# Three more inner fifth products, later sums and another order of the first down pass in a layer of linear attention and gated ReGLU

## Chip, cores and metric

The kernel runs on one core of a Trainium2 chip. The metric is device time in microseconds (us) of one execution; before the change the median of 3 runs is 710.93 us (710.85 to 712.28). The profiled execution took 711.03 us, of which the profile's span is 709.3 us.

## What is computed

`A_x` is 2048 x 1024 in bf16. The layer is a pre-norm linear attention block and a pre-norm feed-forward block, each with a residual:

```
q, k, v = split(layernorm(x) @ wqkv)            # 32 heads of 32
pq, pk  = phi(q), phi(k)                         # phi(t) = where(t > 0, t + 1, exp(t)) + 1e-6
o       = (pq @ (pk^T v)) / (pq @ sum(pk) + 1e-6)
h       = x + o @ wo
n       = layernorm(h)
gate    = n @ W_gate                             # 1024 x 3584
out     = h + (relu(gate) * (n @ W_up)) @ W_down # 3584 x 1024
```

The change touches the feed-forward block alone.

## The kernel before

**Engines and plan.** The program is written as one list of instructions for each engine; a small planner (`_Plan`) adds the semaphore waits from what each instruction reads and writes (`_Buf`; `over` names the buffers that lived at the same address before). Each engine works its list in order. TensorE (PE) multiplies, VectorE (DVE) and ScalarE (ACT) clear PSUM banks and make sums, GpSimd (POOL) makes some sums, SyncE (SP) issues nearly all DMAs.

**Products by sums.** Large products are done by a scheme of the Strassen-Winograd kind: a 2 x 2 block product takes seven block products P1 to P7 instead of eight, with sums of the operands (S1 to S4 of the activations, T1 to T4 of the weights) and sums of the results. A block product here is a stationary 128 x 128 block of weights and 512 moving columns, with four steps of the contraction and two column blocks `u`: 8 matmuls of 512 columns. The same scheme can be used once more inside a block product ("inner"): seven inner products M1 to M7, each 2 matmuls of 256 columns, so 14 matmuls of 256 columns.

**Passes and units.** The tokens are worked in two passes of 1024 (index 0 and 1; "pass 1" in the title of the change is the first one, index 0). A pass has 14 units (`ffn_unit`, line 1728, NPAIR = 14), each of which makes two tiles of the hidden layer (128 rows each) for gate (even unit) or up (odd unit); an odd unit multiplies its result into that of the even unit before it. Then comes a down pass (`down_pass`, line 2033) with W_down.

Inside a unit, two block products can be inner:
- The fifth product P5 (S1 times T1), as M1 to M7, in units of `M0` (line 1722: 4, 6, 8, 10) in the first pass, in all units of the second. It needs sums of quarters of S1 (`x_inner`, once a pass, tile `xs5`) and of T1 (`w_inner`, once a unit, tile `g5`), both in the region RE.
- The first product P1 of the next unit, as R1 to R7 beside the products of this one, if `inner1` of the next unit holds (line 1725); it needs sums of quarters of the raw weights (`w_inner1`, tile `g1`), and VectorE adds Ra at the end. It is left out for unit 0 of both passes and for unit 2 of the first (`NO_R`, line 1723).

VectorE's other work in a unit: the sums T for the next unit (`t_sums`, line 1626: T13, T2, T4, or T1, T2, T4, T3 when split), the evacuations "c22" and "c12" from PSUM, the multiplications h11, h21, h2 of an odd unit, "s5a" of an inner P5. In the first pass it also makes the sums of W_down that the down pass will need (`wd_pair`, line 820, instructions WT; `wl_sums`, line 850, WL, two of whose sums GpSimd makes); they are stored to DRAM (`t_scr`, `r_scr`, `l_scr`). Beside these run, in the first pass, the layer norms of the second half of the tokens (`late_steps`, line 1576: mean, square, norm for each of 8 tiles, on ScalarE with three small GpSimd steps after the square), one or two steps a unit in the places `lna` and `lnb`. The normalised tiles go to DRAM (`n_scr`) and come back transposed: four early, by a DMA transpose in units 11 to 13 into the tile `hnE` (line 286), from where ScalarE copies them into place at the start of the down pass (`early_c`); four in the down pass (`late_t`).

A unit's places are lists of such steps that `ffn_unit` calls between its products: `pre`, `wina`, `winb`, `lna`, `lnb`, `tail`, `mid`, `winc`. They set the order on each engine.

**Down pass.** It has seven products (index `pi` 0 to 6) on sums of the hidden tiles: D1, D2, D3 and D4. D1 is the sum of the second half's columns of an even and an odd tile, D3 the difference of the halves of an even tile (both by `hh_pair`, line 1662, two tiles at a time), D2 = D1 less the first half of the even tile, D4 the first half of the odd tile less D2. In the first down pass products 0 and 2 are direct (`direct`, 56 matmuls of 512 columns), the others are inner ("level two": `level2`, 98 matmuls of 256 columns in seven sets), each with sums of quarters of its own: sg6 for product 1, sg7 for 3, sg5 for 4, sg4 for 5, sg3 for 6. The PSUM banks are used in two halves of four, XB and YB. Weights come through a ring of 7 slots; `load_wd_next` issues the next load on SP when a slot is given back. `ORDER` (line 708) is the order of the weights, the calls of `direct` and `level2` (from line 2271) that of the products, and `at(pi, ci, ...)` places a step behind chunk `ci` of product `pi`.

D1 lives in the region RXH (7 x 1024 columns of 2 bytes, 512 columns a tile), `hnE` before the change in the last half of the eight blocks of RE, where `xs5` and `g5` are too:

```
hnE = RE[:, 4 * D:8 * D].rearrange("p (t a c) -> p t a c", t=STB, c=P)      # line 286
D1  = RXH[:].bitcast(f16).rearrange("p (q t) -> p q t", t=SBW)
```

So before the change no unit after the tenth could use `xs5` and `g5`.

Of the kernel before, what the change touches and what calls it, by code (L numbers as in the profile page):

```python
# [132 lines left out]
def bass_sequential_preLN__linear_attn_block__glu_gated_reglu__prompt_kernel(  # L133
# [71 lines left out]
    with es:  # L205
# [79 lines left out]
        g5 = RE[:, 6 * D:8 * D].bitcast(f16).rearrange("p (s j c) -> p s j c", s=2, j=4)  # L285
        hnE = RE[:, 4 * D:8 * D].rearrange("p (t a c) -> p t a c", t=STB, c=P)
        o0 = (NO + NOE) * D
# [50 lines left out]
        RXH = sb("RXH", [P, (NXN + NHS) * D], bf16)  # L338
        xn = RXH[:, 0:NXN * D].rearrange("p (a b) -> p a b", a=NXN)
        TWo_x = RXH[:, 0:KH * D].bitcast(f16).rearrange("p (j k c) -> p j k c", j=2, k=KH)  # L340

# [239 lines left out]
        for b_ in B_D1:  # L581
            b_.over = B_xn + B_TWo[0::2] + B_hs + hp_x
        for b_ in B_Ef:
# [13 lines left out]
        for b_ in B_hnE:  # L597
            b_.over = B_o + B_oT[0:NOE]
        for b_ in B_hnE:
            b_.over = b_.over + B_xs5 + flat(B_g5)  # L600
        for b_ in B_xs5 + flat(B_g5):
            b_.over = B_o + B_oT[0:NOE]
        for b_ in B_V:
            b_.over = B_hnE
        for b_ in flat(B_hh) + B_out2:
# [1020 lines left out]
        def t_sums(L, eng="dve", split=False):  # L1626
# [30 lines left out]
            if eng == "dve":  # L1657
                return [add13] + add(1, wb(1, 1), tb(0), 0) + add(3, wb(1, 0), tb(1), 1)
            return (add(0, wb(0, 1), wb(0, 0)) + add(1, wb(1, 1), tb(0), 0) + add(2, wb(1, 1), wb(0, 1)) +
                    add(3, wb(1, 0), tb(1), 1))  # L1660

        def hh_pair(q):
            f1, f2, f3 = 2 * q, 2 * q + 1, 2 * q + 4
            t0, t1 = slice(0, SBW), slice(SBW, 2 * SBW)
            PL.add("dve", lambda e: e.tensor_tensor(out=D1[:, q:q + 2, :], in0=hh[:, f1:f3:2, t1],
                                                    in1=hh[:, f2:f3:2, t1], op=ALU.add),
                   reads=[B_hh[f][1] for f in range(f1, f3)], writes=B_D1[q:q + 2], name="D1_%d" % q)
            PL.add("dve", lambda e: e.tensor_tensor(out=hh16[:, f1:f3:2, t1], in0=hh[:, f1:f3:2, t0],
                                                    in1=hh[:, f1:f3:2, t1], op=ALU.subtract),
                   reads=[B_hh[f][0] for f in (f1, f1 + 2)], writes=[B_hh[f][1] for f in (f1, f1 + 2)],  # L1670
                   name="D3_%d" % q)

# [360 lines left out]
        def down_pass(ps_, fill):  # L2033
# [138 lines left out]
            def direct(pi, bk, act_ops, start, evac):  # L2172
                af, ab = act_ops
                for ci, (q0, q1) in enumerate(WCH):
                    def go(ci=ci, q0=q0, q1=q1):
# [119 lines left out]
            sg5 = l2_sums(q_d1, sgs[4], "sg5")  # L2295
            for i in range(4):
                at(1, 2 + i if not last else (2, 3, 4, 5)[i], sg7[i])
            if not last:
                at(0, 0, lambda: d2(0, NH), lambda: d2(NH, NPAIR))
                at(0, 1, sg6[0])  # L2300
                at(0, 2, *sg6[1:3])
                at(0, 3, sg6[3])
                for i in range(4):
                    at(2, 1 + i, sg5[i])
                claim(B_sgg, B_w[0:4])
                at(2, 2, lambda: d4(0, NH))
                for i in range(4):
                    at(2, 1 + i, sg4[i])
                at(3, 0, lambda: d4(NH, NPAIR))
            else:  # L2310
                claim(B_W, B_hnT)
# [340 lines left out]
        for p_ in range(NPASS):  # L2652
            done = []
            for q in range(NPAIR):
# [7 lines left out]
                if (p_, q) == (0, 0):  # L2662
                    pre.append(ss[3])
                if q > 1 and q % 2:
                    wina.append(lambda q=q: hh_pair(q - 3))
                if p_ == 0:
                    raw, lna, lnb, tail = [], [], [], []
                    if q > 0 and ln_q:
# [3 lines left out]
                        lna.append(f_)  # L2672
                        f_, t1 = ln_q.pop(0)
                        lnb.append(f_)
                        done = [t for t in (t0, t1) if t is not None and t < STB]
                    winc = []
# [31 lines left out]
                if q == 0:  # L2708
# [51 lines left out]
            if p_ + 1 < NPASS:  # L2760
# [83 lines left out]
```

## Time and profile before

| | us |
|---|---|
| median of 3 runs | 710.93 |
| profiled execution | 711.03 |
| its span | 709.3 |
| first unit of the first pass begins | 222.62 |
| first down pass begins | 389.05 |
| second pass begins | 466.80 |
| second down pass begins | 631.05 |

All times inside the span count from its start. The beginnings are starts of matmuls in PE's timeline: PE's rows stand in the order of the program, and every unit begins with the first matmul of a known product, so counting the rows of each form cuts the span into units. A window's "x69" counts rows that overlap it, one more than the unit's own 68. In the timeline a row's first number is its start and the second its length, for merged rows the length of all; a matmul's row lasts longer than the distance to the next one, since matmuls are pipelined. "SPq" rows are DMA issues on SP; their length is how long the issue held the queue.

### The profile page before, as it was taken

Reading aid. Unit: us, or ns where it says so; the run is one execution under the profiler, and the core shown is the slowest. Engines: PE = TensorE matmul, PEld = TensorE weight load, DVE = VectorE, ACT = ScalarE, POOL = GpSimd, SP = SyncE. Lnnn points to the kernel's source line nnn. Section 1 sums busy time; section 2 is a strip of 40 time slices with the busy share of each in tenths; the row PEclk is TensorE's granted clock in tenths of the full one; section 3 lists DMA queues with packets and bytes.
Section 4 is the critical chain, followed back from the end, with each engine's and each line's share of the span. In section 5 each row is a group of like instructions: output and inputs, shape, how many; then the busy total and the mean of one; then the engine's idle time right before and its main releaser. Section 6 shows DMA issues by size and latency. Waiting matters only on the chain.

```text
span 709.3 us, 13488 instructions
## 1 busy us (share of the span) xinstructions
PE 704.0 (99%) x5101; PEld 398.3 (56%) x5101; DVE 612.4 (86%) x970; ACT 409.6 (58%) x743; POOL 179.5 (25%) x246
## 2 busy tenths in 40 slices
PE   9999999999999999999999999999999999999998
PEld 4444444444444455555554658865555555568887
DVE  7988867899899899999998787887989888989996
ACT  4887666764863687778785411146666667651010
POOL 3221100114893334243522001321111110000331
PEclk9999999999999999999999999999999999999999
DMA  9852244014999795968899999998465644268996
GB/s 304 255 123 61 39 133 161 29 31 97 231 208 285 233 345 170 304 215 252 271 292 290 310 243 320 315 243 239 133 190 156 193 147 125 87 236 312 345 283 184
DMA packets 170385, 148.80 MB, mean 210 GB/s; under 512 B 54352, under 2 KB 146896, under 8 KB 170320
## 3 DMA queue, kind: packets, MB, share of 16 engines
q1 hardware_dynamic: 165328, 143.35, 67.2%
q0 software_dynamic: 4032, 3.67, 3.5%
q8 instruction: 40, 0.66, 0.4%
q10 hardware_dynamic: 960, 0.92, 0.4%
q14 instruction: 25, 0.20, 0.1%
HBM read 101.97 MB, written 33.88 MB: 192 GB/s over the span
## 4 chain that ended last, share of the span: by engine, by line
PE 93%; DVE 3%; DMA 2%; issue 1%; SPq 0%; DVEq 0%
PE ps L904 93%; DMA RAB<-RXH 1%; DMA RE<-in_A_x_dram 1%; DVE RWG L1152 1%; DVE RC L1127 0%; SPq L655 0%; DVE RE L1776 0%; DVE RW L1127 0%; DVE st L918 0%; DVE RE L991 0%; DVE RXH L1029 0%; DVE RH L1152 0%; DVE RX L1247 0%; DVE RX L988 0%; DVE RE L1688 0%
## 5 line engine op out<-in xcount | busy, mean ns | idle before, releaser
L909 ACT ACTIVATE ps<-ps 128x512 f32<-128x512 f32 (+1 forms) x275 | 138.9, 515 | 181.9 <-PE ps L904 136.4
L904 PE MATMUL ps<-RC,RO 128*128 128x512 f16 (+1 forms) x600 | 141.8, 366 | 0.0
L904 PEld LDWEIGHTS ps<-RC,RO 128*128 128x128 f16 x600 | 58.4, 98 | 49.6 <-ACT ps L909 1.2
L909 ACT ACTIVATE RE<-ps 128x512 f32<-128x512 f32 (+3 forms) x106 | 63.8, 619 | 30.8 <-PE ps L904 12.8
L904 PE MATMUL ps<-RC,RWG 128*128 128x512 f16 x320 | 80.9, 379 | 0.2 <-ACT ps L909 0.2
L904 PE MATMUL ps<-RH,RWG 128*128 128x512 bf16 (+1 forms) x348 | 77.7, 348 | 0.0
L1776 DVE TENSOR_TENSOR RE<-ps,RE 128x1024 bf16<-128x1024 f32 (+1 forms) x46 | 46.6, 1013 | 25.7 <-PE ps L904 23.8
L904 PE MATMUL ps<-RH,RO 128*128 128x512 bf16 (+1 forms) x256 | 65.3, 379 | 0.0
L2060 POOL DMA_DIRECT2D out_dram<-RX x20 | 18.0, 1302 | 150.9 <-DMA RX<-out_dram 75.9
L904 PE MATMUL ps<-RW,RAB 128*128 128x256 f16 (+3 forms) x358 | 52.8, 300 | 0.0
L904 PEld LDWEIGHTS ps<-RH,RWG 128*128 128x128 bf16 x348 | 33.6, 98 | 34.1 <-ACT ps L909 0.3
L904 PE MATMUL ps<-RAB 128*128 128x512 bf16 (+3 forms) x242 | 51.1, 348 | 0.0
L904 PEld LDWEIGHTS ps<-RC,RWG 128*128 128x128 bf16 (+1 forms) x320 | 30.0, 98 | 33.8 <-ACT ps L909 5.1
L904 PEld LDWEIGHTS ps<-RW,RAB 128*128 128x128 f16 (+1 forms) x358 | 34.9, 98 | 14.1 <-DVE RXH L1482 0.5
L806 POOL TENSOR_TENSOR RW<-RW 128x256 f16<-128x256 bf16 x28 | 18.8, 672 | 90.1 <-PE ps L904 70.3
L2051 DVE TENSOR_TENSOR RE<-ps,RE 128x512 f32<-128x512 f32 x46 | 31.6, 686 | 11.3 <-PE ps L904 10.7
L1776 DVE TENSOR_TENSOR RAB<-RAB,RE 128x1024 bf16<-128x1024 bf16 (+1 forms) x43 | 37.4, 872 | 2.0 <-ACT RE L909 1.1
L1776 DVE TENSOR_TENSOR RAB<-ps,RE 128x1024 bf16<-128x1024 f32 x28 | 34.3, 1223 | 5.0 <-PE ps L904 4.7
L1788 ACT ACTIVATE RAB<-RAB 128x1024 bf16<-128x1024 bf16 x28 | 29.5, 1052 | 15.6 <-DVE RAB L1776 15.6
L904 PEld LDWEIGHTS ps<-RH,RO 128*128 128x128 f16 (+1 forms) x256 | 24.4, 98 | 24.6 <-ACT RX L909 1.5
L1644 DVE TENSOR_TENSOR RO<-RWG,RO 128x1024 f16<-128x1024 bf16 x54 | 37.9, 702 | 0.0
L909 ACT ACTIVATE RAB<-ps 128x512 bf16<-128x512 f32 (+2 forms) x54 | 35.6, 659 | 1.6 <-PE ps L904 1.6
(221 smaller groups left out, 1361.4 us busy)
## 6 DMA issues: line engine op xcount, KB each, us to landing
RWG<-in_B_W_gate_dram SPq DMA_DIRECT2D x28, 512.0 KB, 5.7
RWG<-in_B_W_up_dram SPq DMA_DIRECT2D x28, 512.0 KB, 5.3
RW<-l_scr SPq DMA_DIRECT2D x21, 448.0 KB, 5.4
RW<-in_B_W_down_dram SPq DMA_DIRECT2D x14, 512.0 KB, 6.1
l_scr<-RX SPq DMA_DIRECT2D x7, 1024.0 KB, 6.3
RE<-l_scr SPq DMA_DIRECT2D x16, 448.0 KB, 4.7
RW<-t_scr SPq DMA_DIRECT2D x13, 448.0 KB, 5.7
RE<-in_A_x_dram SPq DMA_DIRECT2D x19, 256.0 KB, 3.4
```

The costliest lines, as they stand in the source:

```text
L806: PL.add("pool", lambda e: e.tensor_tensor(out=ly[:, j, :], in0=x[0], in1=y[0], op=ALU.subtract), deps=[PL.prog["pe"][-1]], reads=x[1] + y ...
L904: lambda e: e.matmul(out_ap, lhsT, rhs, start=start, stop=stop, skip_group_check=skip),
L909: PL.add("act", lambda e: e.activation(out=dst, in_=src, func=func), reads=reads, writes=writes, name=name)
L1152: PL.add("dve", lambda e: e.tensor_tensor(out=s(i), in0=in0, in1=in1, op=op), reads=reads, writes=[B_Sx[i][p]], name="Sx%d_%d" % (i + 1, p))
L1644: PL.add(eng, lambda e: e.tensor_tensor(out=tb(j)[0](r), in0=x[0](r), in1=y[0](r), op=ALU.subtract), reads=rd, writes=bt(j, r), name="T%d_ ...
L1776: PL.add("dve", lambda e: e.tensor_tensor(out=dst, in0=in0, in1=in1, op=op), reads=reads, writes=writes, name=name)
L1788: PL.add("act", lambda e: e.activation(out=d, in_=d, func=ACTF.Relu), reads=[], writes=db, name=name)
L2051: PL.add(eng, lambda e: e.tensor_tensor(out=dst, in0=in0, in1=in1, op=op), reads=reads, writes=writes, name=name)
L2060: PL.add("pool", lambda e: e.dma_start(dst, src, accum_op=ALU.add), reads=[bsrc], writes=[B_hscr[st]], slot=sl, name="acc_%d_%d" % (st, dh))
```

## The change

- `M0` gets units 2, 12 and 13: their fifth product is inner. `NO_R` goes: the first product of unit 2 is inner as well.
- `hnE` moves into RXH, over the places of D1 of the last eight tiles (6 to 13), so that `xs5` and `g5` stay free for units 12 and 13.
- D1 and D3 of those eight tiles move out of units 9, 11 and 13 and the end of the pass into the first down pass. D2 is made in two parts.
- The first down pass goes direct (0), direct (2), and then the level-two products 1, 3, 4, 5, 6; product 1 changes from banks YB to XB. The places of its sums are new. In the first chunk of the second direct product the matmuls go bank by bank.
- In the units: `x_inner` moves into unit 0; `w_inner` goes to the front of `tail`, the third WT to its end in units of M0; the last layer-norm steps end a place earlier (unit 11 takes three); the first two down weights are issued in unit 12, two instead of four in unit 13.
- In the second pass GpSimd's sums of W_down (`y_wsums`) get an empty place after every four. The sums S1, S2, S3 for the second pass have other places in the first down pass.

```diff
-        hnE = RE[:, 4 * D:8 * D].rearrange("p (t a c) -> p t a c", t=STB, c=P)
+        hnE = RXH[:, 3 * D:7 * D].rearrange("p (t a c) -> p t a c", t=STB, c=P)
...
         for b_ in B_D1:
-            b_.over = B_xn + B_TWo[0::2] + B_hs + hp_x
+            b_.over = B_xn + B_TWo[0::2] + B_hnE + B_hs + hp_x
...
-        ORDER = [list(range(7)), [0, 2, 1, 3, 4, 5, 6]]
+        ORDER = [[0, 2, 1, 3, 4, 5, 6]] * 2
...
+        def d1_sum(a, b):
+            PL.add("dve", lambda e: e.tensor_tensor(out=D1[:, a:b, :], in0=hh[:, 2 * a:2 * b:2, t1_],
+                                                    in1=hh[:, 2 * a + 1:2 * b:2, t1_], op=ALU.add),
+                   reads=[B_hh[f][1] for f in range(2 * a, 2 * b)], writes=B_D1[a:b], name="D1_%d" % a)
+
+        def d3_sum(a, b):
+            PL.add("dve", lambda e: e.tensor_tensor(out=hh16[:, 2 * a:2 * b:2, t1_], in0=hh[:, 2 * a:2 * b:2, t0_],
+                                                    in1=hh[:, 2 * a:2 * b:2, t1_], op=ALU.subtract),
+                   reads=[B_hh[f][0] for f in range(2 * a, 2 * b, 2)],
+                   writes=[B_hh[f][1] for f in range(2 * a, 2 * b, 2)], name="D3_%d" % a)
...
-        M0 = (4, 6, 8, 10)
-        NO_R = (0, 2)
+        M0 = (2, 4, 6, 8, 10, 12, 13)
+        QD = 6
+        LN3 = (11,)
...
-            return 0 < n < NPAIR and (ps_, n) != NO_R
+            return 0 < n < NPAIR
...
-                            for q in range(q0, q1):
-                                for j in range(STB):
-                                    d_mm(q, j)
+                            jq = [(j, q) for j in range(STB) for q in range(q0, q1)]
+                            if start or ci:
+                                jq.sort(key=lambda x: x[1])
+                            for j, q in jq:
+                                d_mm(q, j)
...
                 direct(0, XB, a_hh(0, 0), True, e_s1)
-                level2(1, YB, q_d2, sgs[1], ev("dU", (U, U)))
                 direct(2, XB, a_hh(1, 0), False, e_11)
+                level2(1, XB, q_d2, sgs[1], ev("dU", (U, U)))
...
-                at(0, 0, lambda: d2(0, NH), lambda: d2(NH, NPAIR))
-                at(0, 1, sg6[0])
-                at(0, 2, *sg6[1:3])
-                at(0, 3, sg6[3])
+                claim(B_sgg, B_w[0:4])
+                at(0, 0, lambda: d2(0, QD))
+                at(0, 4, lambda: d1_sum(QD, NPAIR), lambda: d2(QD, NPAIR))
+                at(2, 0, *sg6[0:2])
+                at(2, 1, *sg6[2:4])
+                at(2, 2, lambda: d3_sum(QD, NPAIR), *sg7[0:2])
+                at(2, 3, *sg7[2:4])
+                at(2, 4, *sg4)
+                at(1, 1, lambda: d4(0, NH))
+                at(1, 2, lambda: d4(NH, NPAIR))
                 for i in range(4):
-                    at(2, 1 + i, sg5[i])
-                claim(B_sgg, B_w[0:4])
-                at(2, 2, lambda: d4(0, NH))
-                for i in range(4):
-                    at(2, 1 + i, sg4[i])
-                at(3, 0, lambda: d4(NH, NPAIR))
+                    at(3, 2 + i, sg5[i])
...
-                if q > 1 and q % 2:
+                if q > 1 and q % 2 and (p_ or q - 3 < QD):
                     wina.append(lambda q=q: hh_pair(q - 3))
...
+                        if q == NPAIR - 2:
+                            lna += [load_wd_next] * 2
+                        if q in LN3 and ln_q:
+                            f_, t0 = ln_q.pop(0)
+                            lnb.append(f_)
...
-                        (tail if q == 0 or q in M0 else winb).append(wds[2])
+                        if q == 0 or q not in M0:
+                            (winb if q else tail).append(wds[2])
...
-                            for _ in range(4):
+                            for _ in range(2):
                                 load_wd_next()
...
                     if q + 1 in M0:
-                        tail += w_inner(q + 1)
+                        tail = w_inner(q + 1) + tail
+                    if q and q % 2 == 0 and q in M0:
+                        tail.append(wds[2])
                     if q + 2 == min(M0):
-                        tail += x_inner()
+                        winb += x_inner()
...
-                    wys = [f_ for m in range(NM) for f_ in y_wsums(m)]
+                    wys = [f_ for m in range(NM) for f_ in y_wsums(m) + [int]]
...
-            hh_pair(NPAIR - 2)
             if p_ == 0:
+                pass
...
             else:
+                hh_pair(NPAIR - 2)
...
-                late += [(nxt_s, (3, 1))] + [(ss[i], ((3, 3), (3, 5), (6, 0), (6, 2))[i]) for i in range(4)]
+                late += [(nxt_s, (1, 5))] + [(ss[i], ((1, 6), (3, 1), (4, 6), (6, 2))[i]) for i in range(4)]
```

More of the change, by code (lines that the diff above doesn't have):

```diff
@@ L597, in bass_sequential_preLN__linear_attn_block__glu_gated_reglu__prompt_kernel @@
         for b_ in B_hnE:
-            b_.over = B_o + B_oT[0:NOE]
-        for b_ in B_hnE:
-            b_.over = b_.over + B_xs5 + flat(B_g5)
+            b_.over = B_xn + B_TWo[0::2] + B_hs + hp_x
         for b_ in B_xs5 + flat(B_g5):
@@ L603, in bass_sequential_preLN__linear_attn_block__glu_gated_reglu__prompt_kernel @@
         for b_ in B_V:
-            b_.over = B_hnE
+            b_.over = B_xs5 + flat(B_g5)
         for b_ in flat(B_hh) + B_out2:
@@ L1660, in t_sums @@
                     add(3, wb(1, 0), tb(1), 1))
-        def hh_pair(q):
[L1663 to L1671, printed above, removed]
+        t0_, t1_ = slice(0, SBW), slice(SBW, 2 * SBW)
+        def d1_sum(a, b):
[7 more added lines that the diff above has]
+                   writes=[B_hh[f][1] for f in range(2 * a, 2 * b, 2)], name="D3_%d" % a)
+        def hh_pair(q):
+            d1_sum(q, q + 2)
+            d3_sum(q, q + 2)
         def w_inner1(ps_, n):
@@ L2295, in down_pass @@
             sg5 = l2_sums(q_d1, sgs[4], "sg5")
-            for i in range(4):
-                at(1, 2 + i if not last else (2, 3, 4, 5)[i], sg7[i])
             if not last:
-                at(0, 0, lambda: d2(0, NH), lambda: d2(NH, NPAIR))
-                at(0, 1, sg6[0])
-                at(0, 2, *sg6[1:3])
-                at(0, 3, sg6[3])
+                claim(B_sgg, B_w[0:4])
[8 more added lines that the diff above has]
+                at(1, 2, lambda: d4(NH, NPAIR))
                 for i in range(4):
-                    at(2, 1 + i, sg5[i])
-                claim(B_sgg, B_w[0:4])
-                at(2, 2, lambda: d4(0, NH))
+                    at(3, 2 + i, sg5[i])
+            else:
                 for i in range(4):
-                    at(2, 1 + i, sg4[i])
-                at(3, 0, lambda: d4(NH, NPAIR))
-            else:
+                    at(1, 2 + i, sg7[i])
                 claim(B_W, B_hnT)
@@ L2672, in bass_sequential_preLN__linear_attn_block__glu_gated_reglu__prompt_kernel @@
                         lna.append(f_)
-                        f_, t1 = ln_q.pop(0)
-                        lnb.append(f_)
+                        t1 = None
+                        if ln_q:
+                            f_, t1 = ln_q.pop(0)
+                            lnb.append(f_)
                         done = [t for t in (t0, t1) if t is not None and t < STB]
+                        if q == NPAIR - 2:
+                            lna += [load_wd_next] * 2
+                        if q in LN3 and ln_q:
+                            f_, t0 = ln_q.pop(0)
+                            lnb.append(f_)
+                            done += [t for t in (t0,) if t is not None and t < STB]
                     winc = []
```

## The prediction

> **What bounds the kernel.** I read the page's shares first, then the chain of waits, then tables of busy time cut at the unit borders, then the timelines of single engines.
>
> ```profile
> PE 704.0 (99%) x5101; PEld 398.3 (56%) x5101; DVE 612.4 (86%) x970; ACT 409.6 (58%) x743; POOL 179.5 (25%) x246
> PEclk9999999999999999999999999999999999999999
> PE 93%; DVE 3%; DMA 2%; issue 1%; SPq 0%; DVEq 0%
> ```
>
> TensorE is the bound: 99% busy at full clock, and the chain lies on it for 93% of the span. So a gain can only come from fewer or shorter matmuls, or from the few places where PE stands still. The table of windows, one line a unit (columns: stretch, length, then busy time of PE, PEld, DVE, ACT, POOL with counts), shows what a unit costs:
>
> ```profile
> 236.24:246.64 10.40, 10.40 (x50) 4.59 (x48) 9.22 (x12) 7.80 (x14) 3.11 (x6) 1.00 0.72 216
> 246.64:260.25 13.61, 13.61 (x71) 6.85 (x70) 12.33 (x16) 9.94 (x17) 5.37 (x6) 1.00 1.06 336
> 343.18:354.87 11.69, 11.69 (x69) 6.62 (x68) 11.10 (x19) 10.09 (x19) 4.52 (x7) 1.00 0.72 227
> 354.87:366.76 11.89, 11.89 (x64) 6.04 (x62) 10.80 (x17) 9.16 (x17) 2.72 (x3) 1.00 0.96 274
> 366.76:378.65 11.89, 11.89 (x64) 6.08 (x63) 11.52 (x16) 9.67 (x17) 6.45 (x7) 1.00 1.15 322
> 378.65:389.05 10.40, 10.40 (x49) 4.60 (x48) 7.54 (x10) 5.73 (x10) 0.00 (x0) 1.00 0.96 274
> 620.89:631.05 10.16, 10.16 (x56) 5.26 (x54) 8.06 (x13) 6.27 (x12) 0.00 (x0) 1.00 0.48 153
> ```
>
> These are units 1, 2, 10, 11, 12, 13 of the first pass and unit 13 of the second. Unit 10 has the inner fifth product, 11 and 12 have not: 11.69 against 11.89 us. Unit 1 does not yet compute its successor's inner first product, unit 11 does.
>
> **The matmuls.** A product is 8 matmuls of 512 columns, or 14 of 256 in seven inner products. In the timeline below, 8 of 512 run from 320.03 to 321.76 (0.216 us each) and a pair of 256 takes 0.22 us: 8 x 0.216 - 14 x 0.109 = 0.20 us saved a product. The windows agree. Unit 1 gains the inner first product of unit 2 and becomes like unit 11 (11.89); unit 2 loses its plain first product, gains the inner fifth and becomes like unit 10 (11.69): 10.40 + 13.61 = 24.01 becomes 23.58, -0.43. Unit 12 becomes like 10: -0.20. Unit 13 becomes like unit 13 of the second pass: 10.40 to 10.16, -0.24. **Together -0.87 us.**
>
> **What the new sums cost on VectorE.** Each is hidden as long as VectorE reaches the next PSUM evacuation in time.
> - Unit 0 gets the four operand sums of S1 (1.54 us by their rows in unit 2, 259.65 to 261.19) ahead of its evacuation "c22", which now waits 0.92 us for PE. It comes 0.5 us later; the product that needs the bank starts 0.67 us after c22's end in the trace. Nothing is lost, 0.2 us is left.
> - Unit 1 gets two sets of quarter sums (1.06 us each: 0.42 + 2 x 0.29 and gaps) and one Ra (0.70). Its c22 moves back 0.85 us, because eight more 256-column matmuls stand before it; with the idle 0.94 that covers 1.06 and the 0.14 carried over. 0.
> - Units 2, 12, 13 get an s5a (0.68), 12 a set of quarter sums behind it; units 9, 11, 13 lose a D1 and a D3 (2 x 0.69). ScalarE trades two s5 copies (0.60) for three of 0.38 and one of 0.6: no wait follows, as in unit 10. 0.
> - The second pass's order of GpSimd sums gets a blank after every four; see the end of this part.
>
> **GpSimd against VectorE.** This is the one place where the stretch pays something back. From units 7 and 8:
>
> ```profile
> 318.31 1.16 POOL L871 TENSOR_TENSOR RX<-RW,RX 128x512 f16<-128x512 f16 x1
> 318.93 0.81 DVE L1688 TENSOR_TENSOR RE<-RO 128x512 f16<-128x512 f16 x1
> 319.30 0.38 PE L904 MATMUL ps<-RC,RO 128*128 128x256 f16 x2
> 319.80 0.11 PEld L904 LDWEIGHTS ps<-RE 128*128 128x128 f16 x2 [0.40 <-DVE RE L1688]
> 320.03 1.89 PE L904 MATMUL ps<-RH,RWG 128*128 128x512 bf16 x8
> 321.76 0.38 PE L904 MATMUL ps<-RE 128*128 128x256 f16 x2
> ```
>
> The first quarter sum takes 0.81 us here and 0.42 elsewhere, because a GpSimd sum is still running beside it (to 319.47); unit 8 stands still for 0.30 us more than unit 10. In units 3, 5 and 9 that GpSimd sum ended 0.1 us before the quarter sum. In unit 7 it was late, as three small GpSimd steps of a layer norm (317.09 to 318.35) stand before it; they follow a square of ScalarE in "lnb". Unit 1 has the same square in lnb, and its successor now opens with quarter sums: **+0.30**. Unit 11 gets a third layer-norm step, again a square in lnb, after a mean that the trace has at 363.27: the square ends near 365.5 and the GpSimd sum (1.45 us after it, as in unit 7) starts near 366.9, against 365.13 now, in the middle of unit 12's quarter sums and of h2. From above: all 1.16 us of it land on VectorE, and T2, which in unit 10 ended 0.16 us before its product, comes late by 1.0. From below: it slips between two instructions, 0. The nearest row is h2 of unit 1 at 246.63 (1.89 us instead of 1.22, beside a GpSimd sum at 246.28): 0.66 late less 0.16 of slack, **+0.50**. The Trainium skill, page "SBUF — State Buffer", section "Who interferes with whom", says that a VectorE instruction with two SBUF inputs and a GpSimd instruction that reads SBUF exclude each other, the second blocking in full until the first ends. The 0.81 us agrees; by that rule unit 12's term would be the upper end, 1.0, and the sum 0.5 higher.
>
> Units 1 and 2 of the second pass took 11.86 and 11.91 us by their matmuls' starts, their like 11.69. There h11 was slowed the same way:
>
> ```profile
> 489.11 0.67 POOL L806 TENSOR_TENSOR RW<-RW 128x256 f16<-128x256 bf16 x1 [4.00 <-DMA l_scr<-RW]
> 489.21 1.11 DVE L1776 TENSOR_TENSOR RAB<-RAB,RE 128x1024 bf16<-128x1024 bf16 x1
> ```
>
> The GpSimd sum waited for the store of the buffer that it refills. With the blank it comes one place later, after h11: 0.17 + 0.22 = **-0.39**.
>
> **The down pass.** The direct units hide the moved sums. VectorE ends h21 3.0 us after the pass begins. Then come D2 for six tiles (2.02 for 3584 columns, so 1.7), D1 for eight (4096 columns, 2.3), D2 (2.3), four sg6 (1.09 each), D3 (2.3), four sg7, four sg4. D1 also waits for the four copies of the normalised tiles, which end 6.1 us in (395.12 now, from 389.05). That makes 6.1 + 2.3 + 2.3 + 4.4 = 15.1 us to the last sum that the first level-two product set needs, and 26.1 for all, against 24.2 us of direct products (2 x 12.09). Only sg4 overruns, and it is wanted four sets later. Without that cover (the old order, 12.1 us after the start) it would cost 3 us. The second direct unit reuses the banks of the first: four ScalarE copies of 0.6 us from about 10.9 us on stay ahead of PE, which goes bank by bank in its first chunk. The first level-two set takes the same banks after four bf16 copies, equally early. 0. The down weights of level-two sets come with 0.46 us to spare at the worst, behind the accumulating stores of the second direct unit; their order relative to that unit stays, so 0.
>
> **The sum.** 711.03 - 0.87 - 0.39 + 0.30 + 0.50 = 710.57 us for the profiled execution (span 709.3, and 1.7 around it). The median of the runs shown is 0.10 below that execution: **710.5 us**.
>
> **Rivals.**
> 1. No new collision (units 2 and 12 run clean): 711.03 - 0.87 - 0.39 - 0.10 = 709.7. For it: units 4, 6 and 10 run clean. Against: the layer-norm steps before the sum. If unit 8's wait also goes, 709.4.
> 2. Both collisions at full weight, and the blank brings nothing: 711.03 - 0.87 + 0.4 + 1.0 - 0.10 = 711.5. For it: the quarter sum's 0.81 us ended 0.28 us after the GpSimd sum, nearly a full block; against: h2 lost only 0.66. The Trainium skill's rule above gives this rival for unit 12.
> 3. **Slower: the down weights come late.** The stores of the last two tiles move behind unit 12's c12 and its sums:
>
> ```profile
> 373.16 0.51 SPq L655 DMA_DIRECT2D t_scr<-RW  x1
> 382.12 1.06 SPq L655 DMA_DIRECT2D RW<-in_B_W_down_dram  x2
> 383.23 0.49 SPq L655 DMA_DIRECT2D l_scr<-RX  x1
> 383.82 5.87 SPq L655 DMA_DIRECT2D RW<-in_B_W_down_dram  x1
> ```
>
> From 15.9 us before the down pass they move to about 8.5 (an even unit's c12 ends 0.5 us before the next unit; then 1.06 + 0.6 + 0.6 of sums; unit 13 lasts 10.2), and SP's queue behind them with them: two transposes, the third and fourth weight load (about 2.6 us before the pass, now 6.9), the 1 MB store and the fifth load, held 5.87 us there. The third load landed 6.5 us after its issue; so 3.9 us in, wanted at 5.1. It decides if landing takes over 7.7 us. If it takes 10.4, as the 1 MB store did (383.23 to 393.63), PE waits 2.7 us: 710.5 + 2.7 = 713.2. Against it: two loads go out ahead of these stores now, and the first 24 us ask for only 384 KB in 2.6 us (12 matmuls).
> 4. The sums of the down pass come late: sg6's first, done near 11.8 us, is wanted at 25.7 (after 24.2 of direct products and a product of 14 x 0.109). The copies before D1 would have to end 14 us later; 2 us more than that makes 712.5.
>
> **Chances.** Forecast (710.0 to 711.0) 0.45, rival 1 0.24, rival 2 0.17, rival 3 0.12, rival 4 0.02. A measurement of this kernel tells about 0.2% (1.4 us) from no change: under 709.5 is faster, which only rival 1 with unit 8's wait gone reaches (0.08); over 712.35 needs rival 3 or 4 (0.14); the rest, 0.78, is no change. Range 709.3 to 711.9: rival 1's lower end and a full rival 2 with 0.4 us of one late load.
>
> **What would show it.** Unit 2 11.7 to 12.1 us and unit 12 11.7 to 12.7, with 32 matmuls of 512 columns gone and 56 of 256 come (5125 in all). A first quarter sum of 0.8 us at the start of units 2 and 12, beside a GpSimd sum, shows the collision; 0.42 refutes it. Units 1 and 2 of the second pass at 11.69 show the blank's gain. PE waiting for a DMA early in the first down pass shows rival 3. I am wrong if PE stands still over 1 us in the down pass, or if the units don't shorten to 11.69 plus a wait that a GpSimd sum explains.

## The result, and the profile after

| | median us | lowest to highest | runs |
|---|---|---|---|
| before | 710.97 | 710.49 to 712.45 | 12 |
| after | 712.62 | 712.14 to 713.8 | 12 |

The ratio over all runs is 1.0021 (95% interval 1.0012 to 1.003; such ratios, here and below, differ a little from the quotient of the two medians): the changed kernel is slower by 1.65 us, where 710.5 was forecast with a range up to 711.9. The profiled execution took 712.65 us, its span is 710.9.

Two lines of the page that were shown of before (busy time, then the chain of waits by engine; the granted clock is 1.00 in every stretch below):

```profile
PE 699.8 (98%) x5072; PEld 401.0 (56%) x5125; DVE 617.1 (87%) x982; ACT 411.8 (58%) x752; POOL 177.5 (25%) x246
PE 88%; DVE 5%; ACT 1%; issue 1%; POOL 0%; DVEq 0%; POOLq 0%; ACTq 0%
```

The weight loads (5125, as forecast) are all recorded, 53 of the matmuls are not. VectorE's share of the chain went from 3% to 5%: more of the chain now lies on VectorE's work, for which PE waits. The table of windows, cut at the borders of units 0, 1, 2, 10, 11, 12, 13 of the first pass, of the first level-two set of the first down pass, and of unit 1 of the second pass (stretch, length, then busy time of PE, PEld, DVE, ACT, POOL with counts):

```profile
222.93:237.36 14.43, 13.57 (x71) 6.78 (x71) 14.29 (x22) 6.96 (x13) 4.77 (x4) 1.00 0.66 229
237.36:249.25 11.89, 11.84 (x63) 6.07 (x63) 11.16 (x16) 9.16 (x18) 4.53 (x6) 1.00 0.75 228
249.25:261.22 11.97, 11.81 (x68) 6.47 (x68) 11.47 (x19) 10.12 (x19) 4.06 (x6) 1.00 0.87 274
344.14:355.83 11.69, 11.64 (x69) 6.59 (x69) 11.10 (x19) 10.09 (x19) 4.52 (x7) 1.00 0.79 245
355.83:367.72 11.89, 11.84 (x63) 6.08 (x63) 9.61 (x15) 10.30 (x19) 2.41 (x5) 1.00 0.93 212
367.72:380.15 12.43, 11.81 (x69) 6.51 (x68) 11.90 (x19) 9.11 (x17) 5.01 (x6) 1.00 1.04 321
380.15:390.31 10.16, 10.11 (x54) 5.28 (x54) 9.00 (x13) 6.26 (x12) 0.00 (x0) 1.00 1.02 236
414.48:425.97 11.49, 10.87 (x100) 9.52 (x99) 9.17 (x9) 2.14 (x4) 3.77 (x4) 1.00 1.01 284
482.34:494.03 11.69, 11.64 (x69) 6.66 (x68) 8.66 (x17) 7.54 (x16) 1.34 (x2) 1.00 0.87 246
```

Set against the same stretches of before, each from the start of its first matmul to the start of the next stretch's, the whole difference is in seven places. Every other unit and product set has the length it had, to 0.01 us.

| stretch | before | after | forecast | measured |
|---|---|---|---|---|
| unit 0 | 13.62 | 14.42 | 0 | **+0.81** |
| units 1 and 2 | 24.02 | 23.86 | -0.43 + 0.30 | -0.16 |
| unit 12 | 11.89 | 12.43 | -0.20 + 0.50 | +0.54 |
| unit 13 | 10.40 | 10.16 | -0.24 | -0.24 |
| first level-two set, first down pass | 10.70 | 11.48 | 0 | **+0.78** |
| fourth product (index 4), first down pass | 10.78 | 10.86 | 0 | +0.08 |
| units 1 and 2 of the second pass | 23.77 | 23.38 | -0.39 | -0.39 |
| sum | | | -0.46 | +1.42 |

The forecast's sum and the measured one differ by 1.88 us, and 1.59 of that is in two places that were costed at nothing. (The first unit began at 222.93 us instead of 222.62, which makes 1.73 for the two traces up to the end of the last product; experiments 1 to 9 show that this start is scatter.)

**Unit 0.** Its timeline from the last operand sum S4 to P4 (start, duration, engine, line, operation, tiles and shapes):

```profile
229.07 3.26 POOL L879 TENSOR_TENSOR RAB<-RW 128x256 f16<-128x256 bf16 x2 [9.82 <-DMA RW<-in_B_W_down_dram]
...
230.11 1.69 DVE L1647 TENSOR_TENSOR RO<-RWG 128x2048 f16<-128x2048 bf16 x1
...
231.72 0.89 DVE L1713 TENSOR_TENSOR RE<-RC 128x512 f16<-128x512 f16 x1
...
232.64 0.42 DVE L1713 TENSOR_TENSOR RE<-RE,RC 128x512 f16<-128x512 f16 x1
232.75 0.84 POOL L879 TENSOR_TENSOR RAB<-RW,RAB 128x256 f16<-128x256 bf16 x1 [0.43 <-PE ps L902]
232.98 0.89 DVE L1713 TENSOR_TENSOR RE<-RC 128x512 f16<-128x512 f16 x1
...
234.13 1.21 DVE L1781 TENSOR_TENSOR RAB<-ps,RE 128x1024 bf16<-128x1024 f32 x1
...
235.63 0.81 PE L902 MATMUL ps<-RH,RO 128*128 128x512 bf16 x3 [0.86 <-DVE RAB L1781]
```

L1713 are the four operand sums moved ahead of c22 (234.13). Two of them take 0.89 us instead of 0.42, each while a GpSimd sum (L879, one of the sums for W_down) is running. T13 before them (230.11) takes 1.69 instead of 1.22 for the same reason. c22 ends at 235.34, and P4 starts at 235.41 instead of 234.60. (The record of its first matmul is missing; the second starts at 235.63, and matmuls of 512 columns follow each other by 0.216 us.)

**Unit 2.** Its first quarter sum begins beside a GpSimd sum that ends at 249.39, and takes 0.79 us instead of 0.42, as forecast:

```profile
248.24 1.15 POOL L869 TENSOR_TENSOR RX<-RW,RX 128x512 f16<-128x512 f16 x1
248.88 0.79 DVE L1692 TENSOR_TENSOR RE<-RO 128x512 f16<-128x512 f16 x1
```

**Unit 12.** The GpSimd sum that the forecast expected near 366.9 us of the old trace is at 367.86, which is the same place 0.97 us later:

```profile
367.80 1.45 DVE L1692 TENSOR_TENSOR RE<-RO,RE 128x256 f16<-128x256 f16 x2
...
367.86 1.24 POOL L869 TENSOR_TENSOR RX<-RW,RX 128x512 f16<-128x512 f16 x1
...
370.31 0.68 DVE L1642 TENSOR_TENSOR RO<-RWG,RO 128x1024 f16<-128x1024 bf16 x1
...
371.05 0.82 PE L902 MATMUL ps<-RC,RO 128*128 128x512 f16 x3 [0.57 <-DVE RO L1642]
```

The two quarter sums of 0.29 us took 1.45 together (the second, from 368.12, took 1.13); T2 (370.31) came late by as much, and P6 (371.05) waited for it.

**The first level-two set.** VectorE's two D4 of 2.02 us stand in it between the first two evacuations into dU and the next three, and M3 (the seventh inner product) at 424.44 behind two of these:

```profile
417.81 1.42 DVE L2056 TENSOR_TENSOR RE<-ps,RE 128x512 f32<-128x512 f32 x2 [1.27 <-PE ps L902]
...
419.14 3.95 DVE L2056 TENSOR_TENSOR RAB<-RAB,RC 128x3584 f16<-128x3584 bf16 x2
...
423.01 2.01 DVE L2056 TENSOR_TENSOR RE<-ps,RE 128x512 f32<-128x512 f32 x3
424.41 1.44 PEld L902 LDWEIGHTS ps<-RW,RO 128*128 128x128 f16 x14 [0.88 <-issue]
424.44 1.69 PE L902 MATMUL ps<-RW,RO 128*128 128x256 f16 x14 [0.62 <-DVE RE L2056]
```

M3 accumulates on the bank that M5 used before; the sum that clears it ended at 424.30. Once the D4 were done, VectorE needed 1.3 us for the two sums waiting there.

**The rest went as forecast.** h11 of unit 1 of the second pass takes 0.68 us again (1.11 before), with the GpSimd sum behind it:

```profile
491.33 0.68 DVE L1781 TENSOR_TENSOR RAB<-RAB,RE 128x1024 bf16<-128x1024 bf16 x1
...
492.38 0.67 POOL L804 TENSOR_TENSOR RW<-RW 128x256 f16<-128x256 bf16 x1 [5.16 <-issue]
```

And the down weights moved as the slower rival said, without being late. SyncE's queue around the start of the down pass (390.31):

```profile
389.37 1.03 SPq L653 DMA_DIRECT2D RW<-in_B_W_down_dram  x2
390.45 0.58 SPq L653 DMA_DIRECT2D l_scr<-RX  x1
391.13 4.71 SPq L653 DMA_DIRECT2D RW<-in_B_W_down_dram  x2
```

The third load, issued at 389.37, landed at 393.93 and was used at 395.49, so 1.56 us were left (5.56 before). The fifth, held behind the 1 MB store at 390.45 until 395.33 (the last row merges it with the sixth), landed with 1.64 us left (5.16 before).

### The profile page after: what moved, and what is told of

The parts are those of the page before. It is cut to its first block, busy times and chain, and to the rows that moved or that the text cites. A ratio compares the mean times of both kernels' runs of the same rounds, so it can differ in the third digit from the quotient of the medians.

```text
span 710.9 us, 13506 instructions
## 1 busy us (share of the span) xinstructions
PE 699.8 (98%) x5072; PEld 401.0 (56%) x5125; DVE 617.1 (87%) x982; ACT 411.8 (58%) x752; POOL 177.5 (25%) x246
## 4 chain that ended last, share of the span: by engine, by line
PE 88%; DVE 5%; ACT 1%; issue 1%; POOL 0%; DVEq 0%; POOLq 0%; ACTq 0%
PE ps L902 88%; DVE RE L1781 1%; DVE RC L1614 1%; DVE RAB L1781 1%; DVE RE L1692 0%; DVE RAB L2056 0%; DVE RE L2056 0%; ACT RXH L942 0%; ACT ps L907 0%; ACT RAB L942 0%; ACT RAB L1559 0%; DVE RO L1647 0%; DVE RE L1713 0%; DVE RX L1713 0%; DVE RXH L1480 0%
## 5 line engine op out<-in xcount | busy, mean ns | idle before, releaser
L907 ACT ACTIVATE ps<-ps 128x512 f32<-128x512 f32 (+1 forms) x283 | 141.9, 511 | 186.8 <-PE ps L902 141.2
L902 PE MATMUL ps<-RC,RO 128*128 128x512 f16 (+1 forms) x588 | 138.7, 364 | 0.6 <-DVE RO L1642 0.6
L1781 DVE TENSOR_TENSOR RE<-ps,RE 128x1024 bf16<-128x1024 f32 (+1 forms) x49 | 48.7, 993 | 27.3 <-PE ps L902 26.5
L902 PE MATMUL ps<-RH,RO 128*128 128x512 bf16 (+1 forms) x228 | 59.4, 379 | 2.3 <-DVE RAB L1781 0.9
```

What stands on the lines that cost most here:

```text
L902: lambda e: e.matmul(out_ap, lhsT, rhs, start=start, stop=stop, skip_group_check=skip),
L907: PL.add("act", lambda e: e.activation(out=dst, in_=src, func=func), reads=reads, writes=writes, name=name)
L1781: PL.add("dve", lambda e: e.tensor_tensor(out=dst, in0=in0, in1=in1, op=op), reads=reads, writes=writes, name=name)
```

## The experiments

Nine kernels ran. The first four are edits of the changed kernel, each timed beside the kernel before (710.97 us in these runs too, 711.07 in those of the ninth).

**1. The first half of D4 one place earlier.**

```
-                at(1, 1, lambda: d4(0, NH))
+                at(1, 0, lambda: d4(0, NH))
```

> The first half of D4 goes one place earlier in the first level-two set of the down pass, ahead of the first two sums of dU. Theory A (the first matmul of product M3 accumulates on the bank that M5 used, and the evacuation of that bank stands behind both halves of D4 on VectorE): the stop of 0.90 us before M3 goes, the set takes 10.70 us instead of 11.48, the kernel 712.62 - 0.79 = 711.8 us (1.0012 of before). Rival B (M3 waits for its down weights, which land only 1.6 us ahead of their use): the set stays at 11.48, the kernel at 712.6. Rival C (VectorE simply has too much to do by then, wherever D4 stands): the stop moves to another product of the same set, 712.4 to 712.7.

712.0 us, ratio 1.0013 (1.0004 to 1.0022). The set takes 10.70 us again, every other stretch what it took after the change. The same place of the timeline:

```profile
416.75 2.02 DVE L2056 TENSOR_TENSOR RAB<-RAB,RC 128x3584 f16<-128x3584 bf16 x1
418.69 1.41 DVE L2056 TENSOR_TENSOR RE<-ps,RE 128x512 f32<-128x512 f32 x2
420.01 2.02 DVE L2056 TENSOR_TENSOR RAB<-RAB,RC 128x3584 f16<-128x3584 bf16 x1
421.94 1.43 DVE L2056 TENSOR_TENSOR RE<-ps,RE 128x512 f32<-128x512 f32 x2
...
423.94 1.69 PE L902 MATMUL ps<-RW,RO 128*128 128x256 f16 x14
```

The first D4 now lies in the 1.27 us in which VectorE stood idle, and M3 (423.94) follows without a stop. Theory A holds; B and C fall, since the weights' loads and the amount of VectorE work were the same.

**2. Unit 0's GpSimd sums later** (`raw` holds the four sums, a place each; `int` is a step that does nothing).

```
+                        if q == 0:
+                            raw = [int, int, lambda r=raw: (r[0](), r[1]()), lambda r=raw: (r[2](), r[3]())]
```

> The four GpSimd sums of unit 0 of the first pass go behind its last two products but one (two behind P7, two behind P3) instead of one behind each of four. Theory A (two of the four operand sums xs and T13 were stretched by the GpSimd sums beside them, which made c22 late): xs1 and xs3 take 0.42 us again, T13 1.22, c22 comes 1.4 us earlier, the stop of 1.12 us before P4 goes, unit 0 takes 13.62 us, the kernel 712.62 - 0.81 = 711.8. Rival B (the four sums are too much for VectorE without any GpSimd beside them): xs 0.42, but at least half of the stop stays, 712.2 or more. Rival C (the GpSimd sums now stretch the sums of unit 1): unit 0 at 13.62, unit 1 above 12.2 instead of 11.89, 712.1 to 712.6.

711.81 us, ratio 1.0009 (1.0 to 1.0018); unit 0 takes 13.62 us, unit 1 11.89. From T13 to P4:

```profile
230.10 1.22 DVE L1647 TENSOR_TENSOR RO<-RWG 128x2048 f16<-128x2048 bf16 x1
231.24 0.42 DVE L1713 TENSOR_TENSOR RE<-RC 128x512 f16<-128x512 f16 x1
...
232.71 1.23 DVE L1781 TENSOR_TENSOR RAB<-ps,RE 128x1024 bf16<-128x1024 f32 x1
232.75 1.30 POOL L879 TENSOR_TENSOR RAB<-RW 128x256 f16<-128x256 bf16 x2 [13.51 <-PE ps L902]
```

The operand sums take 0.42 us each and c22 comes 1.42 us earlier in the unit. With T13 at 1.22 the four sums by themselves are hidden, as the forecast had it; beside GpSimd they are not. The last two lines show a second thing: c22, which reads PSUM and one tile of SBUF, takes its usual 1.23 us with two GpSimd sums running beside it.

**3. The layer norm's square behind the GpSimd sum.**

```
+                    if q in (1, 7, 11):
+                        tail.insert(0, lnb.pop())
```

> In units 1, 7 and 11 of the first pass the last layer-norm step (the square on ScalarE and the three small GpSimd steps after it) is put behind the second GpSimd sum of the weights, which so comes some 1.2 us earlier. Theory A (the sum runs beside the quarter sums of the next unit only because these steps stand before it): the first quarter sum of units 2, 8 and 12 takes 0.42 us, units 2 and 8 take 11.69 us (11.97 and 11.98 now) and unit 12 11.69 (12.43 now), the kernel 712.62 - 0.28 - 0.29 - 0.74 = 711.3. Rival B (unit 12 is late by its third layer-norm step on ScalarE or by the two added s5a and quarter sums, not by GpSimd): units 2 and 8 at 11.69, unit 12 stays above 12.2, 712.0. Rival C (the layer-norm steps are late instead and the transposes behind them stop SP's queue): a new stop in units 3, 9 or 13, 711.6 or more.

711.41 us, ratio 1.0006 (0.9997 to 1.0015). Units 2, 8 and 12:

```profile
249.13:260.82 11.69, 11.64 (x69) 6.62 (x68) 11.10 (x19) 10.09 (x19) 5.62 (x7) 1.00 0.89 287
319.86:331.55 11.69, 11.64 (x68) 6.59 (x68) 11.10 (x19) 10.09 (x19) 5.63 (x7) 1.00 0.87 286
367.02:378.71 11.69, 11.64 (x68) 6.59 (x68) 11.07 (x19) 9.17 (x17) 5.32 (x6) 1.00 1.08 334
```

All three are at the 11.69 us of an undisturbed unit: unit 12 has room for its third layer-norm step, its s5a and its quarter sums once the GpSimd sum is out of the way. Units 3, 9 and 13 did not change. Theory A holds. Unit 8's 0.30 us was there before the change, so this gain goes beyond undoing. Unit 0, which the edit does not touch, took 14.30 us here and 14.42 after the change.

**4. The three edits together.**

> The three edits together. Theory A (three separate stops, none of them hiding another): 712.62 - 0.79 - 0.81 - 1.31 = 709.7 us, 0.9982 of before, so that the change pays what the matmuls and the blank give. Rival B (a gain ahead in the first pass is taken back where the down weights are nearly late, with 1.6 us to spare): the first pass is 2.1 us shorter, but the direct products of the down pass stop for a DMA, 710.2 or more.

709.79 us, ratio 0.9985 (0.9976 to 0.9993): 2.83 us less than the changed kernel (2.91 expected), and less than before by 1.18. By the matmuls' starts, units 0, 1, 2 take 13.62, 11.89, 11.69 us, 12 and 13 take 11.69 and 10.16, the level-two set 10.70, and the two direct units of the down pass 12.09 each, as before: no load came late, with 1.4 us left at the worst (third load). The 0.08 us of the fourth product stayed in every experiment and were not pursued. Rival B falls. From the first unit to the end of the last matmul, the trace is 1.50 us shorter than before's.

**5. The blank alone, on the kernel before.**

```
-                    wys = [f_ for m in range(NM) for f_ in y_wsums(m)]
+                    wys = [f_ for m in range(NM) for f_ in y_wsums(m) + [int]]
```

> The kernel before with one edit: a blank after every four GpSimd sums of the second pass. Theory A (the blank moves the sum that waits for its store behind h11, and that is all it does): units 1 and 2 of the second pass take 11.69 us instead of 11.86 and 11.91, everything else as before, 710.97 - 0.39 = 710.6 us (0.9995). Rival B (the gain needs the other edits, or is given back at the end of the pass, where the sums run out): 711.0. The start of the first unit is read too: it was 222.6 us in the trace of before and 222.9 to 223.2 in the five traces of changed kernels, whose program up to there issues the same matmuls; 222.9 or more here says that this is scatter between executions, 222.6 that the moved buffers cost it.

710.9 us, ratio 0.9996 (0.9987 to 1.0006): the times can't tell. The trace can: units 1 and 2 of the second pass take 11.69 us each, everything else what it took. The first unit began at 223.03 us, in a program that is the old one up to there; over all ten further traces, of the changed kernel and of the nine experiments, it began between 222.70 and 223.35. So the 0.31 us at the start is scatter between executions.

**6. Unit 2 back, its operand sums left where the change puts such sums.**

```
-        M0 = (2, 4, 6, 8, 10, 12, 13)
+        M0 = (4, 6, 8, 10, 12, 13)
...
-            return 0 < n < NPAIR
+            return 0 < n < NPAIR and (ps_, n) != (0, 2)
```

> The changed kernel with unit 2 of the first pass as it was before: no inner first product, no inner fifth, the four operand sums back in unit 2. Theory A (unit 2 costs 0.81 us in unit 0 and 0.27 in the collision with GpSimd, and brings 0.43): units 0, 1 and 2 take 13.62, 10.40 and 13.62 us as before, the kernel 712.62 - 0.81 - 0.27 + 0.43 = 712.0. Rival B (unit 0 is late for another reason, such as the moved buffers of the normalised tiles): unit 0 stays at 14.42, the kernel 712.8.

713.58 us, ratio 1.0033 (1.0021 to 1.0046): neither. Units 0 and 1 are at 13.62 and 10.40 us, so B falls; unit 2 takes 15.13 instead of 13.62. The edit was not the undoing it was meant to be, since the four sums stood at the end of unit 2 before, behind c12, and now stand ahead of its c22. GpSimd sums beside them stretch the first (0.89 us instead of 0.42) and T2 ahead of it (1.16 instead of 0.69). But VectorE also waited for a load earlier in the unit:

```profile
251.88 2.68 DVE L826 TENSOR_TENSOR RW<-RW 128x2048 f16<-128x2048 bf16 x3 [1.00 <-DMA RW<-in_B_W_down_dram]
```

This load of W_down was issued at 243.65 and landed at 251.71, 8.1 us later (6.1 us in experiment 9, where VectorE did not wait for it). So the 1.52 us of unit 2 are not the price of the sums' place alone. Unit 12 took 12.75 us here.

**7. The operand sums in unit 1, ahead of its c22.**

```
-                    if q + 2 == min(M0):
+                    if q + 1 == min(M0):
```

> The changed kernel with the four operand sums (1.54 us) one unit later, in unit 1 ahead of its evacuation c22, and nothing else. Theory A (a sum is hidden only as far as VectorE stands idle before the next evacuation, plus what that evacuation is early): unit 0 takes 13.62 us; in unit 1 VectorE stands idle for 0.48 us ahead of c22, and c22 ended some 0.7 us before its product could use it, so P4 comes 0.35 us late and the sums behind it 1.06 us late, which with the collision of 0.27 makes unit 1 12.2 and unit 2 12.7 us: 712.62 - 0.81 + 0.3 + 0.7 = 712.8. Rival B (only the GpSimd sums matter, VectorE has room): units 0, 1, 2 at 13.62, 11.89, 11.97, 711.8.

713.82 us, ratio 1.0038 (1.0026 to 1.0051). Unit 0 is at 13.62; unit 1 takes 13.24 instead of 11.89, unit 2 11.91. A has the sign and 0.3 + 0.7 us of cost, 1.29 was measured in units 1 and 2, in other places than it said. (Unit 12 at 12.61 us, and units 5 and 6 of the second pass at 11.79 and 11.91, were longer too, which was not pursued.) B falls. The last operand sum shows what A had left out:

```profile
244.74 0.42 DVE L1713 TENSOR_TENSOR RE<-RC 128x512 f16<-128x512 f16 x1
244.79 1.38 POOL L869 TENSOR_TENSOR RX<-RW,RX 128x512 f16<-128x512 f16 x1 [3.06 <-PE ps L902]
245.07 1.38 DVE L1713 TENSOR_TENSOR RE<-RC,RE 128x512 f16<-128x512 f16 x1
...
246.38 1.21 DVE L1781 TENSOR_TENSOR RE<-ps,RE 128x1024 bf16<-128x1024 f32 x1
```

It takes 1.38 us instead of 0.42: it started 0.28 us after a GpSimd sum and ended 0.28 us after it.

**8. The three edits, with the down pass in its old order.** Its core (the first four sums also go ahead of the set, behind D2, and the weights' order becomes the old one):

```
                 direct(0, XB, a_hh(0, 0), True, e_s1)
-                direct(2, XB, a_hh(1, 0), False, e_11)
-                level2(1, XB, q_d2, sgs[1], ev("dU", (U, U)))
+                level2(1, YB, q_d2, sgs[1], ev("dU", (U, U)))
+                direct(2, XB, a_hh(1, 0), False, e_11)
```

> The kernel with the three edits (709.8 us), its first down pass in the order of before: direct, level two, direct, with its first four sums ahead of the first level-two set and the weights loaded in that order. Theory A (the forecast's: without both direct units as cover the last sum that this set needs ends 15.1 us into the pass, and the set begins at 12.1): a stop of up to 3 us, 712.8. Rival B (the set asks for them one by one: M1 takes D2 itself, done at 10.8 us and wanted at 12.1, M7 the first sum, 11.9 against 13.6, M6 the third, 14.0 against 15.1, M3 the last): no stop, 709.8, and the new order is worth nothing by itself. Rival C (the sums are in time, but this set uses its weights faster than a direct unit, and the loads behind the moved stores are late): a stop for a DMA in the first level-two set, 710.3 to 712.

710.64 us, ratio 0.9993 (0.9984 to 1.0002). The set takes 11.30 us, +0.60; no other stretch differs from experiment 4. Neither sums nor weights stop it: the sums end at 400.18, 401.18, 402.30 and 403.43 us, M7, M6 and M3 want the first, third and last at 401.72, 403.25 and later, and each of the set's loads lands 0.86 us or more ahead of its use (M3's weights 0.25 us ahead of where M3 would have begun without the stop). The 0.60 us is the stop of before M3 again:

```profile
406.61 2.02 DVE L2056 TENSOR_TENSOR RAB<-RAB,RC 128x3584 f16<-128x3584 bf16 x1
408.54 2.00 DVE L2056 TENSOR_TENSOR RE<-ps,RE 128x512 f32<-128x512 f32 x3
...
409.96 1.69 PE L902 MATMUL ps<-RW,RO 128*128 128x256 f16 x14 [0.44 <-DVE RE L2056]
```

So B is right about the sums and wrong about the stop: what the new order is worth here is 0.60 us, by the time that VectorE has for D4 between the sums and the evacuations. That reading is argued from the rows; the old order with D4 elsewhere was not tried.

**9. Unit 2 undone to the letter:** experiment 6 with the four sums in `tail`, as before the change.

```
-                        winb += x_inner()
+                        tail += x_inner()
```

> The changed kernel with unit 2 undone to the letter: the four operand sums too are where they were before, behind c12 at the end of unit 2. Theory A (in the last undoing the sums stood ahead of c22 of unit 2, and that place alone cost 1.52 us): units 0, 1 and 2 take 13.62, 10.40 and 13.62 us as before, and all that is left of the change is unit 12 (0.5 to 0.9 over), unit 13 (-0.24), M3 in the down pass (+0.78) and the blank (-0.39): 710.97 + 0.74 - 0.24 + 0.87 - 0.39 = 711.9. Rival B (unit 2 needs that time wherever the sums stand, since something else of the change has moved onto VectorE there): unit 2 above 14.5, 713 or more.

712.11 us, ratio 1.0022 (1.0013 to 1.0032). Units 0, 1 and 2 take 13.62, 10.40 and 13.62 us; unit 12 12.75, 13 10.16, M3's stop and the blank as in the changed kernel. The units came out as Theory A said, and behind c12 the four sums cost nothing. That their place alone cost 1.52 us in experiment 6 is not shown: c22 came 2.13 us later in the unit there than here, and about 1.0 us of that is the wait for the load. With the 0.6 us of slack, about 0.5 us would have reached PE without that wait (an estimate: 2.13 - 1.0 - 0.6), with 0.94 us of blocks by GpSimd sums still in it.

## Why the prediction was wrong

**The matmuls, -0.87: right.** Units 2 and 12 have the length of unit 10 wherever no stop stands in them (experiment 4: 11.69 us), and unit 13 is at 10.16.

**The blank, -0.39: right** to the digit, alone as well (experiment 5).

**"Nothing is lost, 0.2 us is left" (unit 0's operand sums): wrong, +0.81.** The sum took 1.54 us from rows in which nothing ran beside the four sums. It missed that the GpSimd sums of unit 0 run at their new place. c22 came 1.42 us later in the unit than in experiment 2, where these sums are out of the way; that is 3 x 0.47 for T13, the first and the third sum. 0.6 us of it were slack, and 0.81 reached PE. T13's 0.47 had been in the trace of before too, hidden. With the sums at 0.42 and T13 at 1.22 nothing is lost (experiment 2), so the step that failed is not VectorE's load but the durations put into it.

**The down pass, 0: wrong, +0.78.** "Only sg4 overruns, and it is wanted four sets later" came true: the sums ended 26.2 us after the pass began (26.1 forecast). But the question was put to the sums alone. Behind them on VectorE stand D4, moved along with the order, and then the evacuations, and M3 needs the bank that one of these clears. The late sums kept VectorE busy through the second direct unit, where the first half of D4 stood before; now D4 falls into the time when M2 and M5 want their banks emptied. Experiment 1 shows it by one place of one instruction. The statement that the old order "would cost 3 us" compared the last sum with the first product; experiment 8 shows none of that cost.

**Collisions: +0.30 and +0.50 forecast, 0.27 and 0.74 measured.** The place was right, and experiment 3 takes all of it away. (In experiments 6, 7 and 9, which leave unit 12 as it is, it took 12.75, 12.61 and 12.75 us, up to 1.06 above an undisturbed unit; why it varies was not pursued.) Unit 12's term was mis-sized through one reading: h2's 0.66 us was taken as part of a GpSimd sum of 1.16, so that a block in full seemed refuted. What matters is how long the GpSimd sum still had to run when the VectorE instruction began. Put that way, the rows agree (from the timelines; overlap = end of the GpSimd sum less start of the VectorE instruction):

| VectorE instruction | usual | measured | overlap | lost |
|---|---|---|---|---|
| before, quarter sum, unit 8 | 0.42 | 0.81 | 319.47 - 318.93 = 0.54 | 0.39 |
| before, h2 of unit 1 | 1.22 | 1.88 | 247.43 - 246.63 = 0.80 | 0.66 |
| before, h11, second pass | 0.68 | 1.11 | 489.78 - 489.21 = 0.57 | 0.43 |
| after, quarter sum, unit 12 | 0.29 | 1.13 | 369.10 - 368.12 = 0.98 | 0.84 |
| after, third operand sum, unit 0 | 0.42 | 0.89 | 233.59 - 232.98 = 0.61 | 0.47 |
| experiment 7, fourth operand sum | 0.42 | 1.38 | 246.17 - 245.07 = 1.10 | 0.96 |

The loss is the overlap less 0.14 us each time, and the six rows are no selection: in the eleven traces, from 222 to 640 us, 278 VectorE sums with two SBUF inputs begin while a GpSimd sum of 256 or 512 columns runs, and each loses the overlap less 0.14 us, to within 0.03 us, or nothing where the overlap is shorter than that. The small layer-norm steps of GpSimd (128 x 1) do not act so: after the change one ran from 241.21 to 242.55, and the WL sum that VectorE began at 241.23 took its usual 1.23 us.

The loss beside the large sums is a full block, the rule of the Trainium skill, page "SBUF — State Buffer", section "Who interferes with whom", that the prediction set against the row and did not take: VectorE with two SBUF inputs and a GpSimd instruction that reads SBUF exclude each other, and the later one stands until the first ends. The traces agree, but for the 0.14 us and the small steps. By the rule unit 12's term was 1.0, the upper end; 0.74 was measured, because the sum overlapped by 0.98 and not by all of its 1.24, and T2 had 0.1 us of slack. The Trainium skill says in the same section that a VectorE instruction with at most one SBUF input, outside the two-port modes, does not contend; c22 in experiment 2 agrees, 1.23 us beside two GpSimd sums, and so do 296 VectorE sums with a PSUM input that began beside such a GpSimd sum, none of which lost time.

**The rivals.** Rival 1 (no new collision) fell, since units 2 and 12 both collided. Rival 2 had the mechanism of the collisions right (a full block, though of the overlap and not of the whole sum); its other half, a blank without gain, was wrong. Rival 3's loads moved later as it said, but none was late: 1.6 us are left of 5. Its figure for the third load, 3.9 us into the pass, came out at 3.6 partly by luck: the load was issued 0.9 us before the pass and not 2.6, and landed 4.6 us after its issue and not 6.5. Rival 4 asked whether the sums of the down pass come late; they did not, what stood behind them did. No rival had unit 0. Nor did the signs of being wrong catch either place: the stop in the down pass cost 0.78 us, under the 1 us that was named, and unit 0 was not among the units to look at.

## What to carry to other kernels

Before VectorE work is costed at nothing, look at what GpSimd does at the place it is moved to, and add for each VectorE instruction with two SBUF operands the time that a large GpSimd sum, once begun, still has to run. Work ahead of a PSUM evacuation is paid as soon as the slack there is used up: the same four sums cost 0.81 us ahead of c22 of unit 0 beside GpSimd sums, and nothing there without them or behind c12 of unit 2. When work is moved into a stretch that covers it, ask not only when it is wanted itself, but what stands behind it on its engine and which bank that work must empty.

## What was not expected of the hardware

- The block works in the other direction too: GpSimd sums that take 1.30 us for two in experiment 2 took 3.26 in the changed kernel, the first beside S4, the second beside T13 of VectorE.
- The start of the first unit scatters by 0.7 us between executions of a program that is unchanged up to there (222.62 to 223.35), against 1.65 us that this study had to explain. The lengths of units in which nothing stops PE repeat to 0.01 us, so the units told apart what the medians could not. Units with a collision do not repeat so well: unit 12 took 12.43 to 12.75 us in kernels that do not differ there.
